# Agent attention and a max-out layer on one core: own order tables for the last two groups and the groups beside a batch border, and one more group of q turned by DMA

## The chip, the core and the metric

The kernel runs on one core of one Trainium2 chip. The metric is device time in microseconds (us) of one launch. The profile gives a span, from the first to the last instruction of the program; the measured time also holds some 2.7 us around it.

## The reference

Four batches of 12544 tokens with 128 channels go through two stages. The first is attention by way of 49 agents for each batch. The second is a feed-forward layer that takes the maximum of three products.

```python
a2k = softmax(scale * agents @ k.T)          # 49 x 12544, over the tokens
agent_v = a2k @ v                            # 49 x 128
x = softmax(scale * q @ agents.T) @ agent_v  # tokens x 128
h = max(x @ w1, x @ w2, x @ w3)              # tokens x 768
out = h @ w_out                              # tokens x 128
```

## The kernel before

**Tiles and stages.** Tokens stand in tiles of 128, 98 tiles in a batch, 392 in all. Queries go in 49 groups s of eight tiles (GT = 8). A batch ends in the middle or at the end of a group: the tiles of batch b start in group 12, 24 and 36 (`tails`). Keys and values go in groups of nine tiles (KT = 9). The keys of batch 0 are worked off first, alone. The keys of batch b are worked off beside the query groups of batch b - 1, one key group in each query group (`hosting`). The group just ahead of a border (11, 23, 35) hosts no keys. It hosts the tail of the batch instead (`k_tail`): the sum over all keys, its reciprocal, and two products that fold the agents' values into the weights (G, lines 354 to 361). Query group SB = 36 and later have no keys beside them.

**One query group** is a chain of small steps, each with a name that the tables and the prediction use:
- `load`, `cast` (POOL, line 412) and the turning of q into qT: either `qt` (eight transposes on TensorE, line 417) with `qe` (VectorE copies the result, line 422), or `turn_q_dma` (the DMA queue of SP turns it, line 428). Before the change the second way is used in groups 36 to 48 alone.
- `s` (TensorE, line 434) and `ex` (ScalarE exponentials, line 440).
- for each of six columns f of 128: `u` (TensorE, line 460), `a` (ScalarE ReLU into SBUF, line 475), `v` (TensorE, line 460) and `x` (VectorE maximum, line 485). Column 3 is different: `a3` works in place (line 472), `v3` adds to the same PSUM tile, and `x3` is a ScalarE ReLU (line 483).
- for each half o of the group: `lin` (TensorE, line 490), six `oc` (TensorE, line 499, four matmuls each, one for each column) and `sc` (VectorE scales, line 506); then `store` (SP, line 513).
- `sum` and `rec` (lines 448 and 454): the row sums of the softmax.
- of the hosted keys: `ks` (line 255), `ke` (ScalarE, line 260), `kv` (line 266), `ka` (VectorE, line 276), `kx` (POOL, line 283), and the casts of k and v on POOL (lines 223 and 230).
- of a tail: `sum_e` (VectorE, line 328), `total` (TensorE, line 333), `normalise` (VectorE, lines 339 to 342), `prod0` and `prod1` (TensorE line 354, then ScalarE line 361).

**What sets the order.** Nothing reorders at run time. Each step is put on one list by `at` with a key; group s starts at 6.0 * s, and tables of offsets give each step its key. `emit` sorts the list and issues the steps, so that each engine gets its instructions in this order. A step whose inputs are not yet issued, or for which the ring of PSUM tiles is full, is put aside and issued as soon as it can be:

```python
for op in sorted(ops, key=lambda o: o[:2]):
    if not go(op):
        late.append(op)
        continue
```

A very low offset therefore means "as soon as it can". The rings are three double-bank tiles for `u`, `v` and the products ("uv"), and two single-bank tiles for `qt`, `s`, the host tile, and both halves' outputs ("om"). A step that takes a slot waits on the engine that last read it. Table KEY is used for groups 0 to 35 and LATE for 36 to 48.

Of the kernel before, what the change touches and what calls it, by code (L numbers as in the profile page):

```python
# [16 lines left out]
def kernel(  # L17
# [19 lines left out]
    B, N, C = q.shape  # L37
# [6 lines left out]
    GT = 8  # L44
    NT = N // P
# [3 lines left out]
    NQ = B * NT // GT  # L49
    SB = (B - 1) * NT // GT  # L50
    assert NT % 2 == 0 and B * NT % GT == 0


    KEY = {
        "qt": -5.826, "qe": -4.714, "s": -3.397, "ex": -3.144, "ho": -2.653, "ks": -2.585,
        "ke": -1.395, "u0": -1.385, "u1": -0.945, "a0": -0.578, "a1": -0.505, "kv": -0.272,
        "sum": -0.189, "rec": -0.160, "ka": -0.096, "v0": -0.088, "u3": 0.041, "a3": 0.349,
        "x0": 0.448, "v1": 1.119, "v3": 1.156, "x1": 1.388, "u2": 1.556, "x3": 2.207, "u4": 2.461,
        "a2": 2.461, "v2": 2.540, "a4": 2.626, "x2": 2.904, "u5": 3.056, "v4": 3.065, "a5": 3.309,
        "x4": 3.802, "v5": 4.472, "x5": 5.223, "lin0": 6.482, "oc02": 6.840, "oc03": 7.560,  # L60
        "oc04": 8.286, "oc00": 8.460, "oc01": 8.460, "oc05": 8.461, "sc0": 8.860, "lin1": 9.007,
        "oc15": 9.269, "oc10": 9.504, "oc12": 9.761, "oc11": 11.129, "oc13": 11.301,
        "oc14": 11.651, "sc1": 11.652,
    }
    LATE = {
        "oc04": -102.316, "s": -5.143, "ex": -3.890, "ho": -3.007, "u0": -2.479, "sum": -2.401,
        "a0": -2.109, "u1": -1.115, "rec": -0.632, "u2": -0.631, "a1": -0.201, "v1": -0.150,
        "u3": 0.004, "a2": 0.202, "a3": 1.295, "x1": 1.296, "v0": 1.603, "v3": 1.692, "x0": 1.773,
        "v2": 1.787, "x3": 2.014, "x2": 2.121, "u4": 2.761, "u5": 2.826, "a4": 2.857, "v4": 3.484,
        "a5": 3.667, "v5": 3.891, "x4": 4.081, "x5": 4.963, "lin1": 6.405, "oc14": 6.642,  # L70
        "oc12": 6.780, "oc10": 8.128, "oc11": 8.220, "oc15": 8.227, "oc13": 8.498, "sc1": 8.670,
        "lin0": 9.304, "oc01": 9.553, "oc00": 9.686, "oc03": 11.369, "oc02": 11.426,
        "oc05": 11.684, "sc0": 12.804,
    }
    PRODUCT_KEYS = (-6.500, -6.260)

    const = ctx.enter_context(tc.tile_pool(name="const", bufs=1))
    loads = ctx.enter_context(tc.tile_pool(name="loads", bufs=14))
# [11 lines left out]
    def at(key, fn, name=None, needs=(), ring=None, frees=()):  # L90

        ops.append((key, len(ops), fn, name, needs, ring, frees))
# [102 lines left out]
    def keep_busy(times):  # L197
        t = small_tile("m_ps")
        for _ in range(times):
            nc.tensor.matmul(t, ident, busy, start=True, stop=True, skip_group_check=True)  # L200
# [9 lines left out]
    def k_group(b, t0, n, key, s):  # L210

        d = {}
        early = s is None

        def load():
            for name, src in (("k", k), ("v", v)):
                t = d[name] = load_tile()
                nc.sync.dma_start(t[:, :n, :], src[b, t0 * P:(t0 + n) * P, :].rearrange(
                    "(p j) c -> p j c", j=n))
# [69 lines left out]
        if early:  # L289
            g = ("early", t0)  # L290
            at(key - 30, load)
            at(key - 5, cast_k)
            at(key - 4, cast_v)
            at(key, turn_k, ("kt", g), (), "uv", [("kt_out", g)])
            at(key + 0.5, evacuate, ("kt_out", g), [("kt", g)])

            last = [("normalise", 0)] if t0 + n == NT else []
            late = max(0, (key - last_key) / 6 + 2)
            at(min(key + 6.6, last_key + 0.58 + 0.02 * late), scores, ("ks", g), [("kt_out", g)],
               "uv", [("ka", g)] + last)  # L300
            at(min(key + 7, last_key + 0.64 + 0.01 * late), exps, ("ke", g), [("ks", g)])
            done = last_key + (0.6 + 0.1 * late if late >= 1 else 0.55)
            at(min(key + 13.2, done), values, ("kv", g), [("ke", g)])
            at(min(key + 13.6, done + 0.01), add_values, ("ka", g), [("kv", g)])
        else:
            at(key + KEY["ks"] - 22, load)
            at(max(key + KEY["ks"] - 10, last_key - 3.4), cast_k)
            at(max(key + KEY["ks"] - 8, last_key - 3.3), cast_v)
            if s > 1:
                at(max(key + KEY["ks"] - 6.5, last_key - 3.2), turn_k, ("kt_out", s))  # L310
            else:

                turn = 1.2 if s else last_key + 1.05
                at(turn, turn_k, ("kt", s), (), "uv", [("kt_out", s)])
                at(turn + 0.05, evacuate, ("kt_out", s), [("kt", s)])

            at(key + KEY["ks"] if s else KEY["u0"] + 0.6, scores, ("ks", s), [("kt_out", s), ("ho", s)])
            at(key + KEY["ke"], exps, ("ke", s), [("ks", s)])
            at(key + KEY["ke"] + 1.5, add_exps, ("kx", s), [("ke", s)])
            at(key + KEY["kv"], values, ("kv", s), [("ke", s)])  # L320
            at(key + KEY["ka"], add_values, ("ka", s), [("kv", s)])

    def k_tail(b, sum_key, keys, s):
        d = {}
# [60 lines left out]
    def q_group(s):  # L385
# [3 lines left out]
        key = 6.0 * s  # L389
# [29 lines left out]
        def evacuate():  # L419
# [3 lines left out]
            else:  # L423
                nc.scalar.activation(d["qT"].rearrange("p j c -> p (j c)"), d["qT_ps"], AF.Copy)

        def turn_q_dma():
            d["qT"] = work.tile([P, GT, P], BF16, tag="qT", bufs=3, name="qT")
            nc.sync.dma_start_transpose(out=d["qT"], in_=d["qb"].rearrange("p j c -> p (j c)"))
# [83 lines left out]
            for src, r0, r1, m in rows(d["out"]):  # L512
                nc.sync.dma_start(out[r0:r1, :].rearrange("(p j) c -> p j c", j=m), src)

        K = KEY if s < SB else LATE
        new = [("product", tails[s], i) for i in range(2)] if s in tails else []

        def put(name, fn, *needs, ring=None, frees=()):
            at(key + K[name], fn, (name, s), needs, ring, frees)

        old = [(f"v{f}", s - 3) for f in range(NF)] + [("lin0", s - 3), ("lin1", s - 3),
                                                     ("sum", s - 3)] if s >= 3 else []
        if s == 0:
            at(last_key - 29.9, load)
            at(last_key - 3.5, cast)
            at(last_key + 0.82, turn_q, ("qt", 0), (), "om", [("qe", 0)])
            at(last_key + 0.825, evacuate, ("qe", 0), [("qt", 0)])
            at(last_key + 1, scores, ("s", 0), [("qe", 0)], "om", [("ex", 0)])
            at(last_key + 1.01, exps, ("ex", 0), [("s", 0)])
        elif s < SB:  # L530
            at(key + K["qt"] - 20, load)
            at(max(key + K["qt"] - 7, last_key - 3), cast)
            put("qt", turn_q, ring="om", frees=[("qe", s)])
            put("qe", evacuate, ("qt", s), *([("s", s - 3)] if s >= 3 else []))
        else:
            at(key + K["s"] - 24, load)
            at(key + K["s"] - 8, cast)
            at(key + K["s"] - 5.5, turn_q_dma, ("qe", s))
        if s:
            put("s", scores, ("qe", s), ring="om", frees=[("ex", s)])  # L540
            put("ex", exps, ("s", s), *old)
        extra = [("ka", s)] if s in hosting else [("normalise", tails[s + 1])] if s + 1 in tails else []
        if s:
            put("ho", host_tile, ring="om", frees=[("rec", s)] + extra)
        else:
            at(KEY["u0"] - 0.04, host_tile, ("ho", 0), (), "om", [("rec", 0)] + extra)
        put("sum", sums, ("ex", s), ("ho", s),
            *([("ks", s)] if s in hosting else [("total", s)] if s + 1 in tails else []))
        put("rec", recips, ("sum", s))
# [12 lines left out]
        for o in range(2):  # L562
            put(f"lin{o}", lambda o=o: out_linear(o), ("ex", s), *new, ring="om", frees=[(f"sc{o}", s)])
            for f in range(NF):
                put(f"oc{o}{f}", lambda o=o, f=f: out_hidden(o, f), (f"lin{o}", s), (f"x{f}", s))
            put(f"sc{o}", lambda o=o: out_scale(o), ("rec", s),
                *[(f"oc{o}{f}", s) for f in range(NF)], *([("store", s - 3)] if s >= 3 else []))
        at(key + max(K["sc0"], K["sc1"]) + 0.5, store, ("store", s), [("sc0", s), ("sc1", s)])

    def ramp():  # L570

# [15 lines left out]
    last_key = KEY["u0"] - 2  # L587
# [8 lines left out]
    for g, n in enumerate(first_sizes):  # L596
        k_group(0, sum(first_sizes[:g]), n, first_key + 6.0 * g, None)

        if 4 <= g < len(first_sizes) - 5:
            fillers += [(first_key + 6.0 * g + 0.55, 3), (first_key + 6.0 * g + 1.3, 3)]  # L600
    k_tail(0, last_key, (last_key + 0.95, last_key + 1.02), None)
    for key, n in fillers + [(last_key + 0.9, 2), (last_key + 1.1, 2)]:
        at(key, lambda n=n: keep_busy(n), ("busy", key), (), "om", [("busy", key)])
    tails = {b * NT // GT: b for b in range(1, B)}
    hosting = set()
    for b in range(1, B):
        for g in range(NK):
            s = (b - 1) * NT // GT + g
            hosting.add(s)
            k_group(b, g * KT, min(KT, NT - g * KT), 6.0 * s, s)  # L610
    for s, b in tails.items():
        assert s - 1 not in hosting
        k_tail(b, 6.0 * (s - 1) + KEY["ho"] + 0.001, [6.0 * s + PRODUCT_KEYS[i] for i in range(2)], s - 1)
    for s in range(NQ):
        q_group(s)
    ramp()
# [33 lines left out]
```

The softmax here doesn't subtract the row's maximum and nothing guards it: scores larger than these inputs give would overflow.

## Time and profile before

| | |
|---|---|
| time, three runs | 469.22, 469.46, 470.57 us (median 469.46) |
| the profiled execution | 470.23 us; span 467.5 us |
| TensorE busy, matmuls 5478 | 437.3 us |
| VectorE (DVE) busy | 408.3 us |
| ScalarE (ACT) busy | 396.7 us |
| POOL busy | 165.8 us |

A group of instructions on the page is written as line, engine, operation, result and inputs. The idle time behind the bar is that of the engine just before these instructions, with what ended it. TensorE's share tells little, because matmuls overlap and their ends are modelled. The chain of waits, and the timeline of a single group, tell more. From the start of one group's exponentials (line 440) to the next, the trace has these periods: 8.35 us in groups with keys, 7.83 us in groups 37 to 47, and at the three borders 10.94 (group 11), 10.94 (group 23), and 7.58 and 10.39 us (groups 35 and 36). The first group's exponentials start at 45.18 us, the last one's at 448.81 us.

### The profile page before, as it was taken

The page shows a single profiled execution, that of the slowest core. Times are in us where ns is not written, and L with a number is a line of the kernel's source. Part 1 is how long each engine was busy: PE and PEld are TensorE (multiplying, and loading weights), DVE is VectorE, ACT ScalarE, POOL GpSimd, SP SyncE. Part 2 cuts the span into 40 slices and gives each one's busy share as a digit, 9 for nine tenths or more (in the row PEclk, how much of TensorE's full clock was granted, in tenths as well). Part 3 has the DMA queues.
Part 4 walks back from the last instruction along what each step waited for, and adds up shares of the span by engine and source line. Part 5 has one row for each costly group of instructions (what it writes and reads, how often), then busy time and mean ns, then how long its engine had stood idle before and what let it go on. Part 6 is the DMA issues. An engine that isn't in the chain of part 4 may idle for free.

```text
span 467.5 us, 13338 instructions
## 1 busy us (share of the span) xinstructions
PE 437.3 (94%) x5478; PEld 273.4 (58%) x5478; DVE 408.3 (87%) x519; ACT 396.7 (85%) x461; POOL 165.8 (35%) x166
## 2 busy tenths in 40 slices
PE   2398899999999999999989999999989999999996
PEld 2376366666655666666656666666655555555554
DVE  3155699999998999999998999999988999999995
ACT  3267889989898899898989898998989999999992
POOL 3244863644460545535262446353220111010000
PEclk9999999999999999999999999999999999999999
DMA  8999999998987999987986999976365776553512
GB/s 324 397 411 405 408 289 361 315 325 215 328 277 260 285 263 328 304 266 234 314 291 225 286 335 285 275 226 192 126 114 158 215 169 183 150 145 100 105 77 105
DMA packets 79464, 117.75 MB, mean 252 GB/s; under 512 B 53223, under 2 KB 54699, under 8 KB 79403
## 3 DMA queue, kind: packets, MB, share of 16 engines
q1 hardware_dynamic: 79200, 116.80, 81.8%
q8 instruction: 42, 0.69, 0.6%
q14 instruction: 19, 0.16, 0.1%
q10 hardware_dynamic: 203, 0.10, 0.1%
HBM read 78.74 MB, written 25.69 MB: 223 GB/s over the span
## 4 chain that ended last, share of the span: by engine, by line
PE 78%; DMA 10%; DVE 6%; ACT 3%; issue 1%; POOL 0%; SPq 0%; DVEq 0%; ACTq 0%; POOLq 0%
PE uv_ps L460 33%; PE o_ps L499 28%; DMA st<-in_k_dram 7%; PE o_ps L490 6%; DVE r L485 4%; PE m_ps L417 4%; PE m_ps L434 3%; DMA wst<-in_moe_w_dram 2%; ACT a_sb L475 2%; PE m_ps L266 1%; PE m_ps L255 1%; DVE o_sb L506 1%; DMA ag_st<-in_agents_dram 1%; PE m_ps L448 1%; PE uv_ps L354 1%
## 5 line engine op out<-in xcount | busy, mean ns | idle before, releaser
L485 DVE TENSOR_TENSOR r<-uv_ps,a_sb 128x1024 bf16<-128x1024 f32 x245 | 297.3, 1220 | 13.9 <-PE uv_ps L460 4.2
L475 ACT ACTIVATE a_sb<-uv_ps 128x1024 bf16<-128x1024 f32 x245 | 241.3, 1028 | 11.5 <-PE uv_ps L460 11.1
L460 PE MATMUL uv_ps<-e_q,G 49*128 49x512 bf16 (+3 forms) x1248 | 185.5, 368 | 4.8 <-DVE r L485 2.9
L499 PE MATMUL o_ps<-wo_bf,r 128*128 128x128 bf16 x2352 | 176.4, 220 | 0.0
L499 PEld LDWEIGHTS <-r 128*128 128x128 bf16 x2352 | 137.6, 98 | 44.2 <-issue 42.7
L460 PEld LDWEIGHTS <-G 49*128 49x128 bf16 x1248 | 56.1, 93 | 66.3 <-issue 31.9
L283 POOL TENSOR_TENSOR Eacc<-Eacc,e_k 128x441 f32<-128x441 f32 (+1 forms) x30 | 30.5, 1015 | 130.5 <-ACT e_k L260 130.5
L506 DVE TENSOR_TENSOR o_sb<-o_ps,recips 128x512 f32<-128x512 f32 x98 | 67.6, 690 | 9.7 <-PE o_ps L499 6.8
L412 POOL CAST q_bf<-st 128x1024 bf16<-128x1024 f32 x49 | 51.0, 1040 | 70.6 <-DMA qT<-q_bf 68.8
L483 ACT ACTIVATE r<-uv_ps 128x1024 bf16<-128x1024 f32 x49 | 50.1, 1023 | 26.3 <-PE uv_ps L460 26.3
L223 POOL CAST k_bf<-st 128x1152 bf16<-128x1152 f32 (+2 forms) x45 | 50.4, 1119 | 28.9 <-DMA st<-in_k_dram 26.1
L472 ACT ACTIVATE uv_ps<-uv_ps 128x1024 f32<-128x1024 f32 x49 | 49.6, 1013 | 0.3 <-PE uv_ps L460 0.2
L490 PE MATMUL o_ps<-G,e_q 128*128 128x256 bf16 x196 | 38.0, 276 | 1.8 <-DVE o_sb L506 1.8
L230 POOL CAST v_bf<-st 128x1152 bf16<-128x1152 f32 (+1 forms) x33 | 37.5, 1135 | 0.5 <-DMA st<-in_v_dram 0.5
L440 ACT ACTIVATE e_q<-m_ps 128x512 bf16<-128x512 f32 x49 | 29.9, 610 | 0.5 <-PE m_ps L434 0.5
L243 DVE COPY kT<-uv_ps 128x1152 bf16<-128x1152 bf16 (+1 forms) x14 | 9.9, 709 | 17.9 <-PE uv_ps L237 17.7
L228 ACT ACTIVATE v_bf<-st 128x1152 bf16<-128x1152 f32 (+1 forms) x12 | 12.9, 1072 | 14.6 <-DMA st<-in_v_dram 14.6
L490 PEld LDWEIGHTS <-e_q 128*128 128x128 bf16 x196 | 12.8, 97 | 20.6 <-issue 20.6
L417 PEld LDWEIGHTS <-q_bf 128*128 128x128 bf16 x288 | 16.2, 98 | 14.8 <-issue 13.2
L422 DVE COPY qT<-m_ps 128x1024 bf16<-128x1024 bf16 x35 | 23.8, 681 | 0.0
L417 PE MATMUL m_ps<-ident,q_bf 128*128 128x128 bf16 x288 | 22.2, 220 | 0.8 <-POOL q_bf L412 0.8
L237 PE MATMUL uv_ps<-ident,k_bf 128*128 128x128 bf16 x116 | 11.7, 262 | 10.8 <-POOL k_bf L223 10.8
(68 smaller groups left out, 234.7 us busy)
## 6 DMA issues: line engine op xcount, KB each, us to landing
st<-in_q_dram SPq DMA_DIRECT2D x46, 512.0 KB, 4.6
out_dram<-o_sb SPq DMA_DIRECT2D x46, 512.0 KB, 3.5
st<-in_k_dram SPq DMA_DIRECT2D x40, 576.0 KB, 6.6
st<-in_v_dram SPq DMA_DIRECT2D x40, 576.0 KB, 7.4
st<-in_k_dram SPq DMA_DIRECT2D x3, 512.0 KB, 6.3
st<-in_v_dram SPq DMA_DIRECT2D x3, 512.0 KB, 7.1
wst<-in_moe_w_dram SPq DMA_DIRECT2D x3, 384.0 KB, 10.4
st<-in_q_dram SPq DMA_DIRECT2D x2, 384.0 KB, 4.2
```

The lines of the kernel that those rows point to most:

```text
L223: nc.gpsimd.tensor_copy(out=d["kb"][:, :n, :], in_=d["k"][:, :n, :])
L230: nc.gpsimd.tensor_copy(out=d["vb"][:, :n, :], in_=d["v"][:, :n, :])
L412: nc.gpsimd.tensor_copy(out=d["qb"], in_=d["q"])
L417: nc.tensor.transpose(t[:, j * P:(j + 1) * P], d["qb"][:, j, :], ident)
L460: nc.tensor.matmul(t[:, h, j0 * P:j1 * P], G[b][h * H:h * H + A, col + f * P:col + (f + 1) * P], d["e"][h * H:h * H + A, j0 * P:j1 * P], s ...
L472: nc.scalar.activation(u, u, AF.Relu)
L475: nc.scalar.activation(a_sb[f], u, AF.Relu)
L483: nc.scalar.activation(r, v_ps[f], AF.Relu)
L485: nc.vector.tensor_tensor(out=r, in0=v_ps[f], in1=a_sb[f], op=ALU.max)
L490: nc.tensor.matmul(t[:, i * 2 * C:(i + 1) * 2 * C], d["e"][:, jj * P:(jj + 1) * P], G[batch[jj]][:, C1O:C1O + 2 * C], start=(i == 0), stop ...
L499: nc.tensor.matmul(t[:, c:c + C], r_sb[f][:, h, jj * P:(jj + 1) * P], wo_bf[:, f, :], start=False, stop=True, skip_group_check=True)
L506: nc.vector.tensor_tensor(out=d["out"][:, j:j + m, :], in0=d["o", o].rearrange("p (j c) -> p j c", c=C), in1=d["r"][:, j:j + m].unsqueeze( ...
```

## The change

Three more tables are added: BORDER for the group ahead of a border (11, 23, 35), BEGIN for the group that starts a batch (12 and 24; group 36 keeps LATE), and LAST for groups 47 and 48. The numbers in KEY, LATE and PRODUCT_KEYS are replaced as well. The group ahead of a border has its q turned by the DMA queue, so three groups of `qt` and `qe` go and three DMA transposes come. Loads, casts and turns get fixed offsets instead of offsets that hang on the table, and steps after a cast name it as a need.

```diff
-    PRODUCT_KEYS = (-6.500, -6.260)
+    BORDER = {
+        "sc1": -68.143, "a4": -63.861, "oc05": -59.505, "x0": -20.368, "s": -5.286, "ex": -4.229,
...
+    }
+    BEGIN = {
+        "ex": -67.488, "oc14": -39.744, "oc10": -36.235, "sc0": -20.962, "sc1": -10.161,
...
+    }
+    LAST = {
...
+        "lin1": 6.380, "oc12": 6.800, "oc10": 7.661, "oc14": 9.630, "oc13": 13.661,
+        "oc15": 16.540, "sc1": 27.567, "lin0": 39.242, "oc00": 45.984, "oc03": 53.964,
+        "oc02": 58.314, "oc04": 63.552, "oc05": 93.035,
+    }
+    PRODUCT_KEYS = (-7.059, -3.008)
+
+    def table(s):
+        if s >= NQ - 2:
+            return LAST
+        if s + 1 in tails:
+            return BORDER
+        return BEGIN if s in tails and s < SB else KEY if s < SB else LATE
...
-            at(key + KEY["ks"] - 22, load)
-            at(max(key + KEY["ks"] - 10, last_key - 3.4), cast_k)
-            at(max(key + KEY["ks"] - 8, last_key - 3.3), cast_v)
+            at(key - 24.6, load)
+            at(max(key - 12.6, last_key - 3.4), cast_k, ("k_cast", s))
+            at(max(key - 10.6, last_key - 3.3), cast_v, ("v_cast", s))
...
+        K = table(s)
+        q_dma = s >= SB or s + 1 in tails
...
-        elif s < SB:
-            at(key + K["qt"] - 20, load)
-            at(max(key + K["qt"] - 7, last_key - 3), cast)
-            put("qt", turn_q, ring="om", frees=[("qe", s)])
+        elif not q_dma:
+            at(key - 26, load)
+            at(max(key - 12.8, last_key - 3), cast, ("q_cast", s))
+            put("qt", turn_q, ("q_cast", s), ring="om", frees=[("qe", s)])
             put("qe", evacuate, ("qt", s), *([("s", s - 3)] if s >= 3 else []))
         else:
-            at(key + K["s"] - 24, load)
-            at(key + K["s"] - 8, cast)
-            at(key + K["s"] - 5.5, turn_q_dma, ("qe", s))
+            at(key - 32, load)
+            at(key - 14.3, cast)
+            at(key - 12.3, turn_q_dma, ("qe", s))
```

## The prediction

> **What bounds the kernel now.** I read the chain of waits first, then one period in the timeline, then the places where the period is longer.
>
> ```profile
> PE 78%; DMA 10%; DVE 6%; ACT 3%; issue 1%; POOL 0%; SPq 0%; DVEq 0%; ACTq 0%; POOLq 0%
> ```
>
> TensorE carries the chain, but it is not alone. Group 18 on ScalarE:
>
> ```profile
> 203.75 1.01 ACT L472 ACTIVATE uv_ps<-uv_ps 128x1024 f32<-128x1024 f32 x1
> 205.30 1.02 ACT L483 ACTIVATE r<-uv_ps 128x1024 bf16<-128x1024 f32 x1 [0.54 <-PE uv_ps L460]
> 206.22 1.94 ACT L475 ACTIVATE a_sb<-uv_ps 128x1024 bf16<-128x1024 f32 x2
> ```
>
> Here a3 must end before v3, and v3 before x3: ScalarE idles 0.54 us in each group. The 8.35 us of a group are one loop: a4 ends and frees the slot of v4; TensorE then runs v4, 12 output matmuls, ks, v5 and u0 (1.55 us from v4 to u0); a0 follows 0.42 later; then a0, a1, a3, the wait for v3, x3, a2, a4. Spacings from the trace: 0.05 + 1.55 + 0.42 + 0.92 + 1.00 + 1.01 + 0.05 + 0.49 + 0.92 + 0.90 + 1.03 = 8.34. The border is longer (busy time by stage: TensorE, its weight loads, VectorE, ScalarE, POOL):
>
> ```profile
> 224.73:233.09 8.36, 8.36 (x110) 5.32 (x108) 8.02 (x11) 7.63 (x11) 3.09 (x3) 1.00 0.98 353
> 241.41:252.35 10.94, 9.88 (x108) 5.42 (x108) 9.29 (x14) 9.06 (x11) 1.00 (x1) 1.00 0.73 241
> ```
>
> No engine is full in the second row. ScalarE waits for first products, and these for slots that VectorE frees late, because `normalise` stands in its queue and waits for `total`:
>
> ```profile
> 242.25 1.02 ACT L475 ACTIVATE a_sb<-uv_ps 128x1024 bf16<-128x1024 f32 x1 [0.21 <-PE uv_ps L460]
> 243.99 1.02 ACT L475 ACTIVATE a_sb<-uv_ps 128x1024 bf16<-128x1024 f32 x1 [0.72 <-PE uv_ps L460]
> 245.39 1.02 ACT L475 ACTIVATE a_sb<-uv_ps 128x1024 bf16<-128x1024 f32 x1 [0.37 <-PE uv_ps L460]
> ...
> 243.00 0.48 DVE L339 RECIPROCAL m_ps<-m_ps 128x49 f32<-128x49 f32 x1 [0.41 <-PE m_ps L333]
> ```
>
> The end, VectorE and then TensorE:
>
> ```profile
> 458.38 2.36 DVE L485 TENSOR_TENSOR r<-uv_ps,a_sb 128x1024 bf16<-128x1024 f32 x2
> 460.66 0.68 DVE L506 TENSOR_TENSOR o_sb<-o_ps,recips 128x512 f32<-128x512 f32 x1
> 463.15 0.69 DVE L506 TENSOR_TENSOR o_sb<-o_ps,recips 128x512 f32<-128x512 f32 x1 [0.94 <-PE o_ps L499]
> ...
> 461.61 1.50 PE L499 MATMUL o_ps<-wo_bf,r 128*128 128x128 bf16 x24
> ```
>
> The last maximum x5(48) ends at 460.74. After that only 24 output matmuls stand before the last scaling.
>
> And the start, POOL and then TensorE:
>
> ```profile
> 45.05 1.15 POOL L230 CAST v_bf<-st 128x1152 bf16<-128x1152 f32 x1 [0.48 <-DMA st<-in_v_dram]
> 47.71 1.15 POOL L223 CAST k_bf<-st 128x1152 bf16<-128x1152 f32 x1 [1.52 <-DMA st<-in_k_dram]
> 48.80 1.04 POOL L412 CAST q_bf<-st 128x1024 bf16<-128x1024 f32 x1
> ...
> 48.07 0.39 PE L266 MATMUL m_ps<-e_k,v_bf 128*128 128x49 bf16 x9 [0.69 <-ACT e_k L260]
> ```
>
> **What the Trainium skill says.** TensorEngine Tiling (Array Packing), Key Properties: changing the tiling mode drains TensorE. The trace agrees: output matmuls start 0.056 us apart, a `u` or `v` after one starts 0.151 later, so a switch costs 0.095. TensorE: Matmul & The Clock Gate, "Wait — 56ns, not 53.3ns?", gives the same 56 ns. DMA: Bandwidth & Descriptors, "Anatomy of one DMA — SWDGE (gpsimd) path", puts most of a transfer's fixed time after the last byte; the stores here go from SP, and agree: the last one is issued at 463.86, its packets run from 464.6 to 466.15, the span ends at 467.5.
>
> **Part 1: KEY and LATE, no cost.** In the changed program's order, ScalarE and VectorE do the same steps in the same order in groups with KEY. On TensorE `s, lin1, u5, v4` becomes `s, u5, lin1, v4`: one switch more, 0.095. It is hidden, because v4 waits 0.15 for the end of a4 today. ks moves behind 12 output matmuls instead of 4, 8 x 0.056 = 0.45 later: ke can then start 1.60 us after ex, a0 0.43 later at 2.03, and a0 waits for u0 until 2.15 anyway. That cover is 0.12. LATE drops two switches (oc03 no longer splits u1 from u2), 0.19 of TensorE, but its loop of 7.83 also goes through ScalarE and VectorE (u0 waits for a4, a2 for x5), with the same steps between: nothing.
>
> **Part 2: the start, +0.8.** Because last_key rises from -3.385 to -3.067, the cast of k of group 1 now stands ahead of the cast of v of group 0 in POOL's queue. It still waits for its load until 47.71, and v(0) is cast at 47.71 + 1.09 = 48.80 to 49.95 instead of 45.05. kv(0) needs it: 50.01 instead of 48.07, and queued behind it on TensorE are sum(0), v0(0), u3(0). q of group 1 is cast 1.09 later too, so qt(1) starts at 50.99 instead of 49.90. a3(0) is 1.3 late. Group 1 has waits of its own, and one filler matmul fewer ahead of kv(1); followed step by step a3(1) comes at 59.95 instead of 59.18, and 0.77 stays.
>
> **Part 3: the borders, -4.3.** Removed in each: eight transposes (0.45 on TensorE) and a copy (0.68 on VectorE, line 422). Added: one DMA transpose, 1.6 us in SP's queue (the stores and loads behind it have over 10 us of room) and 4.4 us to landing, by the 13 that the trace has; it is cast and issued over ten key units, 14 us, ahead of `s`. Moved: sum_e ahead of x1 and normalise ahead of sc0, ex of the border group into the 0.54 gap ahead of x3, prod1 behind the next group's ex. Before, total stood behind v4 and normalise waited for it; now it is free at 6.99 us after ex(22) and VectorE reaches it at 7.10. I followed each step with the trace's spacings, in us after ex(22), before from the trace and after by the sum:
>
> - a0(23): 10.90, now 10.03. u0 waits for x2(22), which ends at 9.56, +0.05 +0.42.
> - a1(23): 12.30, now 11.12 (12 output matmuls between u0 and u1).
> - a3(23): 14.97, now 13.19. prod0 alone is ahead of it; u3 waits for x5(22), 12.63.
> - ex(24): 19.26, now 17.51. Then prod1, 0.69, ahead of a5(23).
> - a0(24): 21.42, now 20.07. This is where the normal loop goes on: -1.35.
>
> Groups 11 and 23 have the same order. At group 35, ex(37) comes 26.30 after ex(34) today and 24.7 by the same sum: -1.6. Together -4.3. Late next is u0(23), behind x2(22).
>
> **Part 4: the end, +2.9.** LAST puts lin0 and all oc0 of groups 47 and 48 behind both groups' oc1. lin0 takes a slot of the om ring that sc1 frees. oc10(47) alone now stands ahead of u4(48), which moves a4 0.2 and x5(48) 0.15 earlier, to 460.59. VectorE then does sc1(47) from 460.50 to 461.18 and sc1(48) from 461.11 to 461.80. lin0(48) starts at 461.85 and oc01(48) at 462.07; 44 matmuls x 0.056 remain, the last at 464.48; 0.26 later sc0(48) could start, but sc0(47) stands before it (464.51, spacing 0.61), so it runs from 465.12 to 465.81 instead of 463.84: +1.97. store(47) is issued 0.6 ahead of store(48), where today 2.5 us lie between them. One store's packets fill the 16 DMA engines for 1.6 us, so the second one ends about 1.0 later. No overlap of two stores is in the trace; the bounds are 0 and 1.6. I take 0.95.
>
> **The sum.** 0 + 0.8 - 4.3 + 2.9 = -0.6. Against the profiled execution's 470.23 us (span 467.5) this is 469.6; the median of the runs is 0.77 lower, so I say **468.9 us**. A difference of 0.3% (1.4 us) is about what a measurement of this kernel can tell from no change.
>
> **The rivals.**
> - The gain at the borders comes whole and the end costs less: stores overlap freely (-0.95), and the loop takes up the start's delay (-0.8): -2.35, 467.1 us. For it: the two groups after the start have idle time on both engines. Against: from group 2 on nothing is left to catch up with.
> - The loop slows with KEY (slower). ke stands just ahead of a0 and has 0.12 of cover. Thirty groups use KEY; if ks gives its result d us later than I count, each costs d - 0.12. It decides against the gain from 0.07 a group on (2.1 in all, +1.5, 471.0 us); at 0.15 it gives +3.9, 473.4 us. For it: x4, x5 and u1 hang on the same slots. Against: TensorE reaches v5 at the same time.
> - The borders give little: the tail's steps wait in another place, say u0(23) behind x2(22), and a third of 4.3 remains: +2.3, 471.8 us. Slots are short there; but ScalarE idles 1.3 us today.
> - q by DMA does nothing by itself: the turn is out of the way in both forms and the gain is all order. This changes no number; bounds -0.6 to 0 a border.
>
> **How the numbers follow.** The forecast has 0.52 and lies within 0.3%. The first rival has 0.28, faster. The two slower ones have 0.10 each, 0.20. The range takes in the first rival's end and the slow ones' beginning: 467.0 to 471.0 us.
>
> **What would show it.** In the profile after: periods of 8.35 and 7.83 as before; ex(23) between a3(22) and x3(22); ex(22) to ex(24) 17.5; cast of v(0) at 48.8 and kv(0) at 50.0; 52 matmuls of lines 490 and 499 behind the second-last pair of scalings, and the span's end 5 us or so after they end. Periods of 8.45 in the KEY groups, or borders over 18.5, would make it wrong.

## The result, and the profile after

The changed kernel takes 472.56 us (median of four runs, 472.45 to 472.86) against 469.64 us before on the same chip: a ratio of 1.006, with an interval from 1.0043 to 1.0078. It is slower, by 0.6%. The profiled execution took 472.59 us with a span of 470.8 us, 3.3 us more than the 467.5 us before. The times of these two executions differ by only 2.4 us, because 1.8 us of the time lie outside the span here and 2.7 lay outside it before. 468.9 us had been forecast.

The starts of the exponentials of each group (line 484 now, 440 before) show where the 3.3 us lie. Each row compares the two traces over one stretch.

| stretch | before | after | difference | forecast |
|---|---|---|---|---|
| start of the span to ex(2) | 63.46 | 65.88 | +2.4 | +0.8 |
| first two borders, ex(10) to ex(15) and ex(22) to ex(27) | 44.33, 44.34 | 43.90, 43.88 | -0.43, -0.46 | -1.35 each |
| third border, ex(34) to ex(38) | 34.15 | 32.78 | -1.37 | -1.6 |
| groups 38 to 47 | 78.48 | 78.60 | +0.1 | 0 |
| groups with keys away from the borders | 8.35 | 8.35 | +0.6 in all, see below | 0 |
| ex(48) to the end | 18.73 | 21.18 | +2.45 | +2.9 |

The fifth row is no slower loop. Single groups last longer once (8.66 in group 8, 8.65 in 16, 8.58 in 30; before, one of 8.63 in group 31), and all others keep 8.35. The period of the last groups is 7.86 instead of 7.83; before, a single group of 7.98 lay among them.

The line of the chain by engine, from the page:

```profile
PE 70%; DVE 11%; DMA 10%; issue 5%; ACT 3%; POOL 1%; DVEq 0%; SPq 0%; POOLq 0%; ACTq 0%
```

TensorE fell from 78 to 70%, VectorE rose from 6 to 11%, and "issue", time in which an engine waited for nothing that the profile shows, rose from 1 to 5%.

**The start.** POOL's timeline (start, duration, line, operation; the bracket is the idle time ahead of it and what ended it):

```profile
47.52 1.15 POOL L264 CAST k_bf<-st 128x1152 bf16<-128x1152 f32 x1 [3.20 <-DMA st<-in_k_dram]
48.61 1.15 POOL L271 CAST v_bf<-st 128x1152 bf16<-128x1152 f32 x1
```

As forecast, k of group 1 is cast first. POOL waits 3.2 us for its load, and v of group 0 follows at 48.6. TensorE's timeline at the same place:

```profile
46.72 0.40 PE L296 MATMUL m_ps<-agT,kT 128*128 128x49 bf16 x9
49.81 0.41 PE L307 MATMUL m_ps<-e_k,v_bf 128*128 128x49 bf16 x9 [2.70 <-POOL v_bf L271]
50.94 1.03 PE L458 MATMUL m_ps<-ident,q_bf 128*128 128x128 bf16 x8
51.77 0.63 PE L625 MATMUL o_ps<-busy,ident 128*128 128x512 bf16 x1
```

kv(0) starts at 49.81, near the forecast 50.01. What the forecast had not is in the last two lines: eight transposes take 1.03 us and a filler matmul 0.63. The same two before took 0.62 and 0.38:

```profile
49.90 0.62 PE L417 MATMUL m_ps<-ident,q_bf 128*128 128x128 bf16 x8 [0.53 <-POOL q_bf L412]
50.36 0.38 PE L582 MATMUL o_ps<-busy,ident 128*128 128x512 bf16 x1
```

The transposes start 107 ns apart instead of 56, and the next instruction comes 427 ns behind the filler, where 216 lay between two fillers before. TensorE's granted clock on record agrees (stretch, its length, TensorE's busy time and matmuls, the clock, DMA share, GB/s):

```profile
47.12:50.53 3.41, 0.72 (x17) 1.00 1.04 414
50.53:53.94 3.41, 3.41 (x26) 0.50 1.01 404
```

TensorE ran at half its clock for 3.41 us.

**The border.** Stages from ex(22) to ex(24) and from ex(24) to ex(25) (length; busy time of TensorE, its weight loads, VectorE, ScalarE and POOL with their instructions; clock, DMA share, GB/s):

```profile
235.67:253.18 17.51, 16.90 (x203) 10.79 (x202) 16.48 (x23) 16.02 (x20) 7.25 (x7) 1.00 0.93 300
253.18:262.86 9.68, 8.78 (x134) 6.33 (x131) 8.31 (x11) 8.23 (x11) 3.72 (x4) 1.00 0.96 297
```

The first stage is the forecast 17.51 to the digit. The second one is 1.3 us longer than a group with keys, and both ScalarE and TensorE are idle for a part of it. TensorE:

```profile
255.81 0.84 PE L543 MATMUL o_ps<-wo_bf,r 128*128 128x128 bf16 x12
257.55 0.39 PE L307 MATMUL m_ps<-e_k,v_bf 128*128 128x49 bf16 x9 [0.90 <-POOL v_bf L271]
257.88 0.61 PE L504 MATMUL uv_ps<-e_q,G 49*128 49x256 bf16 x8
```

VectorE, and then ScalarE:

```profile
256.70 0.69 DVE L550 TENSOR_TENSOR o_sb<-o_ps,recips 128x512 f32<-128x512 f32 x1
257.31 0.20 DVE L498 RECIPROCAL recips<-m_ps 128x8 f32<-128x8 f32 x1
```

```profile
258.59 1.01 ACT L516 ACTIVATE uv_ps<-uv_ps 128x1024 f32<-128x1024 f32 x1 [0.91 <-PE uv_ps L504]
```

kv(24) starts 0.05 us after rec(24) ends on VectorE at 257.50. v0 and u3 stand behind kv on TensorE, and a3 on ScalarE waits for u3. The bracket at kv names POOL's cast of v. That can't be the reason. The instructions of the tile v_bf, in the stretch from 255 to 259 us, have this line (its second part gives the first and the last start):

```profile
L307 PEld LDWEIGHTS <-v_bf x9: 95/96/98, 256.4 to 257.7; 128*128 128x128 bf16 x9
```

The first weights of kv(24), which are v, were loaded at 256.4, so that v was there 1.1 us before kv ran. The cast named in the bracket happens to end at the right moment and belongs to a later group.

**The end.** VectorE, and then TensorE:

```profile
458.93 2.36 DVE L529 TENSOR_TENSOR r<-uv_ps,a_sb 128x1024 bf16<-128x1024 f32 x2 [0.55 <-PE uv_ps L504]
461.20 1.28 DVE L550 TENSOR_TENSOR o_sb<-o_ps,recips 128x512 f32<-128x512 f32 x2
465.19 1.29 DVE L550 TENSOR_TENSOR o_sb<-o_ps,recips 128x512 f32<-128x512 f32 x2 [2.70 <-PE o_ps L543]
```

```profile
462.75 2.62 PE L543 MATMUL o_ps<-wo_bf,r 128*128 128x128 bf16 x44
```

The forecast picture: two scalings, 52 matmuls of lines 534 and 543 (the last 44 in one row), two more scalings, and then both stores.

### The profile page after: what moved, and what is told of

Same layout as the page of the kernel before. It is cut to its first block, busy times and chain, and to the rows that moved or that the text cites. A ratio compares the mean times of both kernels' runs of the same rounds, so it can differ in the third digit from the quotient of the medians.

```text
span 470.8 us, 13304 instructions
## 1 busy us (share of the span) xinstructions
PE 435.8 (93%) x5450; PEld 279.2 (59%) x5454; DVE 405.9 (86%) x516; ACT 397.3 (84%) x461; POOL 165.6 (35%) x166
## 4 chain that ended last, share of the span: by engine, by line
PE 70%; DVE 11%; DMA 10%; issue 5%; ACT 3%; POOL 1%; DVEq 0%; SPq 0%; POOLq 0%; ACTq 0%
PE uv_ps L504 29%; PE o_ps L543 24%; DVE r L529 9%; DMA st<-in_k_dram 7%; PE o_ps L534 5%; PE m_ps L458 4%; PE m_ps L478 3%; ACT a_sb L519 2%; DMA wst<-in_moe_w_dram 2%; PE m_ps L307 2%; PE m_ps L296 1%; DVE o_sb L550 1%; DMA ag_st<-in_agents_dram 1%; POOL v_bf L271 1%; PE o_ps L625 1%
## 5 line engine op out<-in xcount | busy, mean ns | idle before, releaser
L543 PE MATMUL o_ps<-wo_bf,r 128*128 128x128 bf16 x2352 | 169.1, 220 | 0.0
L504 PEld LDWEIGHTS <-G 49*128 49x128 bf16 x1248 | 59.3, 93 | 62.9 <-issue 35.2
L458 PEld LDWEIGHTS <-q_bf 128*128 128x128 bf16 x264 | 15.2, 99 | 13.3 <-issue 11.7
L301 ACT ACTIVATE e_k<-m_ps 128x441 bf16<-128x441 f32 (+1 forms) x33 | 17.9, 544 | 4.6 <-PE m_ps L296 1.5
L463 DVE COPY qT<-m_ps 128x1024 bf16<-128x1024 bf16 x32 | 21.8, 680 | 0.0
```

What stands on the lines that cost most here:

```text
L458: nc.tensor.transpose(t[:, j * P:(j + 1) * P], d["qb"][:, j, :], ident)
L504: nc.tensor.matmul(t[:, h, j0 * P:j1 * P], G[b][h * H:h * H + A, col + f * P:col + (f + 1) * P], d["e"][h * H:h * H + A, j0 * P:j1 * P], s ...
L543: nc.tensor.matmul(t[:, c:c + C], r_sb[f][:, h, jj * P:(jj + 1) * P], wo_bf[:, f, :], start=False, stop=True, skip_group_check=True)
```

## The experiments

Each kernel is the changed one with one edit, unless it is said otherwise. Ratios are to the kernel before, run on the same chip. Where two kernels are set against each other, the difference of their ratios is taken times 470 us.

**1. The cast of v(0) first again (e1_cast).**

```diff
-            at(max(key - 12.6, last_key - 3.4), cast_k, ("k_cast", s))
+            at(max(key - 12.6, last_key - (3.25 if s == 1 else 3.4)), cast_k, ("k_cast", s))
```

> The changed kernel, but the cast of v of group 0 stands ahead of the cast of k of group 1 in POOL's queue again. Theory A (the order of these two casts costs the start 2.4 us: kv(0) comes 1.9 us late, and TensorE, idle for 2.9 us ahead of it, then runs at half its clock): ex(1) starts 2.4 us earlier, at about 55.2, matmuls behind kv(0) stand 56 ns apart, and the time is 470.1 us. Theory B (only the lateness of kv(0) costs, as in the prediction's sum; the rest of the 2.4 comes from the other moves at the start): 0.8 us less, 471.8 us, with ex(1) at 56.8. Theory C (the start is taken up later): the time stays at 472.5 us.

Measured: 470.29 us, ratio 0.9999 (0.9984 to 1.0013). That is 0.6%, or 2.9 us, less than the changed kernel: Theory A by the time. But in the profiled execution, one of the slower ones of this kernel (471.67 us), ex(1) came at 56.80, and the transposes again stood 107 ns apart. Nine of the twelve times lay from 469.7 to 470.4 us, three from 471.4 to 472.1. So the order of the casts costs about what was thought, but the clock halves in some executions with the old order too.

**2. Fillers in the idle time (e2_fill).**

```diff
+    at(-0.3, lambda: keep_busy(12), ("busy", -0.3), (), "om", [("busy", -0.3)])
     hosting = set()
```

> The changed kernel with the late cast kept, and with twelve more filler matmuls of 512 columns (2.6 us of TensorE) put into the 2.9 us in which TensorE waits for kv(0). Nothing else moves. Theory A (half of the start's loss is the halved clock after the idle time): behind kv(0) the matmuls stand 56 ns apart instead of 107, a3(0) stays at 51.1, ex(1) comes 1.3 to 1.6 us earlier than 57.57, and the time is about 471.1 us. Theory B (lateness alone): the spacing may change, but ex(1) and the time do not (472.5 us); or kv(0) is pushed back a little and it gets 0.2 us worse.

Measured: 471.35 us, ratio 1.0022 (1.0009 to 1.0035), 1.8 us less than the changed kernel. ex(1) came at 56.32, 1.25 us earlier (1.48 if both are counted from ex(0)). TensorE's timeline:

```profile
47.18 2.75 PE L240 MATMUL m_ps<-busy,ident 128*128 128x512 bf16 x12
50.86 0.62 PE L458 MATMUL m_ps<-ident,q_bf 128*128 128x128 bf16 x8
51.32 0.38 PE L625 MATMUL o_ps<-busy,ident 128*128 128x512 bf16 x1
```

Transposes and filler have their old durations again. Work that nobody needs made the kernel faster: Theory A. kv(0) is as late as in the changed kernel (49.88), so the lateness that is left and the clock are told apart.

**3. LATE for the last two groups (e3_last).** The function `table` returns LATE instead of LAST for groups 47 and 48.

> The changed kernel, but groups 47 and 48 take their order from LATE like the groups ahead of them. Theory A (the 52 matmuls and the second pair of scalings behind the last maximum cost 2.45 us): ex(48) to the end of the span takes 18.7 us instead of 21.2, and the time is 470.1 us. Theory B (most of the loss at the end lies in the two stores that fall together): the matmuls go, but the stores still end within 1 us of before, and only 1.2 us come back, 471.3 us. Theory C (LAST gains something ahead of the end that LATE loses): under 1 us.

Measured: 470.71 us, ratio 1.0008 (0.9994 to 1.0021), 2.4 us less. From ex(48) to the end it takes 18.92 us instead of 21.18. The last two scalings of VectorE:

```profile
464.11 0.69 DVE L550 TENSOR_TENSOR o_sb<-o_ps,recips 128x512 f32<-128x512 f32 x1 [0.56 <-PE o_ps L543]
465.67 0.69 DVE L550 TENSOR_TENSOR o_sb<-o_ps,recips 128x512 f32<-128x512 f32 x1 [0.87 <-PE o_ps L543]
```

They stand apart again, and behind the last one only one store is left. Theory A.

**4. kv ahead of the row sums in groups 12 and 24 (e4_kv).**

```diff
-        "sum": -1.769, "u0": -1.331, "ke": -1.267, "a0": -1.234, "u1": -0.905, "rec": -0.514,
+        "sum": -0.341, "u0": -1.331, "ke": -1.267, "a0": -1.234, "u1": -0.905, "rec": -0.514,
```

> The changed kernel, but in groups 12 and 24 the row sums stand behind kv in TensorE's queue. Theory A (kv waits for rec, which reads the PSUM tile that kv writes, and rec waits behind x5 and sc1 on VectorE; this holds up v0, u3 and with them a3): the wait of 1.1 us ahead of kv(24) goes, a3(24) starts 0.9 us earlier, the same in group 12, and the time is 470.7 us (-1.8). Theory B (the wait moves on: x5 and sc1 are late anyway, and u3 or v0 wait for their slots instead): a3(24) gains under 0.3 us and the time stays within 0.6 us of 472.5. Theory C (rec itself comes later and holds the next group): slower than 472.5.

Measured: 471.28 us, ratio 1.0016 (1.0004 to 1.0028), 2.1 us less. The same two stages as above:

```profile
236.38:253.89 17.51, 16.89 (x203) 10.79 (x202) 16.49 (x23) 16.02 (x19) 7.26 (x7) 1.00 0.91 294
253.89:262.60 8.71, 8.71 (x134) 6.30 (x131) 8.17 (x11) 8.17 (x11) 3.72 (x4) 1.00 0.92 285
```

The second one is 0.97 us shorter, and TensorE is busy through all of it. TensorE, and then POOL:

```profile
257.20 0.39 PE L307 MATMUL m_ps<-e_k,v_bf 128*128 128x49 bf16 x9
257.44 0.24 PE L492 MATMUL m_ps<-sel,e_q 128*128 128x2 bf16 x4
```

```profile
257.12 1.15 POOL L271 CAST v_bf<-st 128x1152 bf16<-128x1152 f32 x1
```

kv no longer waits, and it runs more than 1 us before the cast ends that the bracket had named. The wait was for rec. Group 12 gives the same 0.98 us (8.71 instead of 9.69). Theory A.

**5. All three edits (e5_all).** The edits of e1_cast, e3_last and e4_kv together.

> The changed kernel with all three edits at once: cast of v(0) first again, LATE for groups 47 and 48, row sums behind kv in groups 12 and 24. Theory A (the three losses stand one behind the other on the path and add up; what is left is the gain at the borders): the ratios to the kernel before that each edit alone gave lie 0.6, 0.5 and 0.4% under that of the changed kernel, so the ratio is 0.990 to 0.992, some 466 us; borders together 4.3 us shorter than before. Theory B (the end or the start gives back what the borders gain): ratio 0.995 or more.

Measured: 465.82 us, ratio 0.9908 (0.9893 to 0.9923), span 464.0 us. Faster than both kernels, by 0.9% against the one before. ex(10) to ex(15) takes 42.91 us, ex(22) to ex(27) 42.92, ex(34) to ex(38) 32.77: 1.42, 1.42 and 1.38 under before, 4.2 together. The losses add up: Theory A.

**6. The same with six fillers (e6_fill5).**

```diff
+    for key, n in ((-0.3, 3), (0.17, 3)):
+        at(key, lambda n=n: keep_busy(n), ("busy", key), (), "om", [("busy", key)])
```

> The kernel with the three edits, and three filler matmuls of 512 columns (0.65 us) ahead of kv(0) and three ahead of qt(1), in the two idle stretches of 0.9 and 0.7 us that TensorE has there although the cast of v(0) stands first. Theory A (in some executions these stretches are enough to halve the clock, as in the profiled one with the cast alone put back, where ex(1) came 1.9 us late): ex(1) comes at about 55.0 with matmuls 56 ns apart in between, the times scatter less, and the median falls by 0.3 to 0.8 us against the three edits without fillers. Theory B (stretches under 1 us do not halve the clock; the scatter has another cause): the same time, or 0.2 us more because the fillers hold an output slot.

Measured: 466.22 us, ratio 0.9913 (0.9899 to 0.9926), no difference from 0.9908. ex(1) came at 55.58, 0.5 us later than without the fillers (55.08). The clock halved in neither profiled execution. Where there is no halving to prevent, the fillers only take time. By the granted clock on record, one of the four executions of e5_all probably had a halved start (0.995, 466.52 us) and none of e6_fill5. With so few, nothing decides between the two theories.

**7. The turn by DMA alone (e7_turn).** The kernel before, with one condition changed:

```diff
-        elif s < SB:
+        elif s < SB and s + 1 not in tails:
```

> The kernel before with one part of the change alone: q of groups 11, 23 and 35 is turned by the DMA queue instead of by TensorE and VectorE; all tables stay. Theory A (the turn is out of the way at the border in both forms, the gain there is all order): the three borders change by under 0.2 us each and the ratio to the kernel before is 0.999 to 1.000. Theory B (the eight transposes and the copy stand on the path of the border): 0.4 to 0.7 us less at each border, ratio 0.996 to 0.997.

Measured: 468.68 us, ratio 0.996 (0.9947 to 0.9973). Each border is 0.43 us shorter (10.51 instead of 10.94 twice, 7.15 instead of 7.58): Theory B. VectorE, and then TensorE; ex(22) is at 233.87 here:

```profile
240.95 0.69 DVE L506 TENSOR_TENSOR o_sb<-o_ps,recips 128x512 f32<-128x512 f32 x1
```

```profile
241.69 0.38 PE L490 MATMUL o_ps<-G,e_q 128*128 128x256 bf16 x2
```

Without the copy of line 422 (0.68) ahead of it, this scaling starts 7.08 us after ex(22) instead of 7.68. lin0 takes the slot that the scaling frees. TensorE had idled 0.60 us for it before and does not wait now.

**8. KEY at the borders (e8_key).** `table` returns KEY up to group 35 and LATE from there to 46; groups 47 and 48 keep LAST.

> The changed kernel without the tables BORDER and BEGIN: the groups on both sides of a border use KEY (LATE from 36 on); the turn of q by DMA, the new places of the two products and everything else stay. Theory A (the order of the tables makes the gain at the borders): the stretch from ex(22) to ex(27), 43.9 us in the changed kernel, 44.3 in the one before and 42.9 with the wait of kv gone, grows to 44.0 to 44.6; all three borders lose 1.5 to 2.5 us together, time 474 to 475 us. Theory B (the turn by DMA and the places of the products make it): the stretch stays at 43.9 or gets shorter, because kv does not wait for rec in KEY's order, time 471 to 472.5 us.

Measured: 478.60 us, ratio 1.0171 (1.0157 to 1.0185). ex(22) to ex(27) takes 45.39 us, ex(34) to ex(38) 35.95. Theory A has the right sign, and was too small: the borders lose 6.2 us against the changed kernel, not 1.5 to 2.5. ScalarE at the second border waits for the first product:

```profile
248.10 1.02 ACT L400 ACTIVATE G<-uv_ps 128x1024 bf16<-128x1024 f32 x1 [2.28 <-PE uv_ps L393]
```

This kernel also says something on the start. The casts stand as in the changed kernel, kv(0) waits as long, and yet TensorE's timeline has

```profile
51.24 0.62 PE L456 MATMUL m_ps<-ident,q_bf 128*128 128x128 bf16 x8
51.69 0.38 PE L623 MATMUL o_ps<-busy,ident 128*128 128x512 bf16 x1
```

with full clock. This execution was the fastest of its kernel (477.56 us, mean granted clock 1.000; the others 478.55 to 478.9, 0.993 to 0.994).

**9. The changed kernel once more (e9_again).**

> The changed kernel itself once more, with more executions. Theory A (whether the clock halves behind the late kv(0) differs from execution to execution, since with the same late cast it halved in three profiled executions and not in a fourth): the times spread over two to three levels between about 469.5 and 473 us; if the profiled one is not halved, ex(2) minus ex(0) is about 19.7 us instead of 20.96, with matmuls 56 ns apart. Theory B (the 2.9 us of idle time halve it every time): all times within 0.5 us of 472.5, and 107 ns apart in the profile again.

Measured: 472.80 us, from 471.35 to 474.24, ratio 1.0048 (1.003 to 1.0067). The profiled execution was the slowest; its clock was halved for 6.83 us, and ex(2) came 22.24 us after ex(0). The spread is as Theory A has it, but the level of 469.5 us that it names was set too low: at full clock the late kv(0), the wait of kv and the end still cost what they cost. The fastest execution, 471.35 us, is the one with a mean granted clock of 0.999; the other five have 0.990 to 0.996. With the ratio measured here in place of 1.006, the gains of experiments 1 to 4 would each be 0.6 us smaller (2.3, 1.2, 1.9 and 1.5 us). That is how far the times can be trusted; the stretches of the traces agree far better with each other (43.87 to 43.90 us at each of the first two borders in all five traces that keep the changed order there).

**10. KEY at the borders, products at their old places (e10_keyprod).** As e8_key, with PRODUCT_KEYS = (-6.500, -6.260).

> The changed kernel without BORDER and BEGIN, and with the two products of a border back at the places of the kernel before (-6.5 and -6.26). Theory A (the tables' net effect at the first two borders is nothing beyond the turn by DMA; the 1.5 us lost there with KEY and the products' new places came from those places): ex(22) to ex(27) takes 43.9 to 44.1 us, ex(34) to ex(38) about 33.7, the time is 472.5 to 474 us. Theory B (KEY's order is bad at a border in itself): ex(22) to ex(27) stays above 45 us, time over 476 us.

Measured: 486.07 us, ratio 1.0333 (1.0314 to 1.0352); ex(22) to ex(27) takes 47.23 us. The size is that of Theory B. ScalarE at the second border:

```profile
248.10 1.05 ACT L517 ACTIVATE a_sb<-uv_ps 128x1024 bf16<-128x1024 f32 x1
252.57 1.02 ACT L400 ACTIVATE G<-uv_ps 128x1024 bf16<-128x1024 f32 x1 [3.42 <-PE uv_ps L393]
```

The new KEY has a0 at 0.133 and a1 at 0.192, where the old one had -0.578 and -0.505. The products' copies into G stand at -0.5 and -0.26 on the same scale. So the new KEY puts them ahead of a0 and a1 of the border group, and ScalarE, which takes its steps in order, waits 3.42 us for the product. In e8_key the first product stands at -1.06, also ahead of a0, and the wait was 2.28. Behind the wait TensorE's clock halved as well: for 6.8 us at the first border (from 146.8), for 3.4 at each of the other two (from 256.0 and 361.8) and for 3.4 at the end (from 471.0). So 486.07 us holds both losses, and they are not told apart. KEY with both products behind a0 and a1 was not tried: shown is that the new KEY loses with the products at these two places, not that it must lose at a border.

**The start in all traces.** From ex(0) to ex(2), in us, by the order of the two casts and by the spacing of the transposes of k of group 1:

| | 56 ns apart | 107 ns apart |
|---|---|---|
| v(0) first | 18.28 (before), 18.14 (e5_all), 18.55 (e6_fill5, with fillers) | 19.65 (e1_cast), 19.49 (e7_turn) |
| k(1) first | 19.72 (e8_key), 19.48 (e2_fill, with fillers) | 20.96 (after), 20.78 (e10_keyprod), 22.07 (e3_last), 22.29 (e4_kv), 22.24 (e9_again) |

The late kv(0) by itself costs 1.2 to 1.6 us. The halved clock costs another 1.1 to 1.5 where it lasts for 3.41 us, or 2.4 to 2.8 where it lasts for 6.83 (e3_last, e4_kv, e9_again).

How often it halves can be estimated from the mean granted clock of each execution, which is on record: 3.41 us at half clock lower the mean of a span of 470 us by 0.0036. (The clock also falls behind the last matmuls, where it no longer costs anything, so each execution's span is read beside it.) The twenty executions of e3_last fall into three groups: 0.998 (four, 468.9 to 469.7 us), 0.994 to 0.996 (nine, 470.3 to 470.9) and 0.992 (seven, 471.2 to 472.0). Read in this way, the clock halved in 44 of the 51 executions with k(1) first and no fillers at the start (after, e3_last, e4_kv, e8_key, e9_again), in one of nine with fillers (e2_fill), and in 6 of 21 with v(0) first (e1_cast, e5_all, e7_turn). Of the 49 executions of the kernel before that ran beside experiments 1 to 4, 23 have 0.995 or less. Its profiled execution does not, which is a part of why the two profiles differ by more than the medians.

## Why the prediction was wrong, point by point

- **Part 1, KEY and LATE without cost: right for the loop with keys.** The period with KEY is 8.35, so the cover of 0.12 us ahead of a0 held, and the first slower rival (a loop of over 8.42) fell. What was put at nothing came to 0.7 us all the same: 0.1 in groups 38 to 47 (7.86 against 7.83) and 0.6 in single long groups, whose cause is open.
- **Part 2, the start: right path, wrong size.** v(0) was cast at 48.61 (forecast 48.8), and kv(0) came at 49.81 (50.01). a3(0), forecast 1.3 us late, came 1.4 us late (51.10 instead of 49.72). The step that failed is "0.77 stays". The sum let group 1 take up 0.5 of the 1.3. At full clock nearly nothing is taken up: counted from ex(0), a3(0) is 1.3 us late in e2_fill and 1.55 in e8_key, and a3(1) still 1.2 and 1.45. The sum also priced every later matmul with the spacings of a warm TensorE, and the halved clock added the rest. a3(1) came at 61.61, where 59.95 had been forecast, and the term of 0.8 measured 2.4. The Trainium skill (TensorE: Matmul & The Clock Gate, "What's actually happening") says that TensorE falls to half its clock after an idle window of about 3.4 us, that the window runs freely, and that the moment varies between runs. The prediction used that page for a spacing and did not ask whether the 1.9 us that it added to an idle time of 0.9 came near such a window.
- **Part 3, the borders: right to a1(24), then a wait was missed.** ex(24) came 17.51 us after ex(22) (17.51), a0(24) 20.04 (20.07). The step that failed is "this is where the normal loop goes on". BEGIN puts sum(24) ahead of kv(24); in KEY it is behind. kv writes the PSUM tile that rec reads, so now it waits for rec, and rec stands behind x5(23) and sc1(22) on VectorE. This took back 0.97 of some 1.42 us in each of groups 12 and 24 (e4_kv). Without it, e5_all has -1.42, -1.42 and -1.38, 4.2 us together, where 4.3 had been forecast. Group 36 uses LATE and hosts no keys, so the third border kept its gain in the changed kernel too.
- **Part 4, the end: right, a little large.** The second pair of scalings ends 16.86 us after ex(48) (465.19 + 1.29 - 449.62) instead of 15.03: +1.83, where 1.97 had been forecast. The stores take the other 0.62 of the 2.45, where 0.95 had been taken between bounds of 0 and 1.6. e3_last gives back 2.26 of it.
- **The rivals.** "The borders give little" (471.8 us) came nearest, in part by luck. Its mechanism was of the right kind, a step that waits in another place, but u0(23) was not the place, and half of the gain remained (2.3 of 4.3) instead of a third; the dearer start made up for it. "q by DMA does nothing by itself" was wrong: it is worth 0.43 at each border, within its bounds of 0 to 0.6. The changed kernel gains no more than this at the first two borders (43.89 in e7_turn, 43.90 and 43.88 after), because the wait of kv takes back what the tables BORDER and BEGIN add to it there. Without them the new KEY loses, at least with the products at the two places tried (e8_key, e10_keyprod).
- **The sum.** Measured 2.4 - 2.3 + 2.45 + 0.7 (single long groups and the last groups) = 3.3, as the spans have it; forecast 0.8 - 4.3 + 2.9 = -0.6. Of the difference of 3.9, some 2.0 are the wait of kv, 1.6 the start, and 0.7 the single and the last groups; the end gave 0.45 back.

## What to carry to other kernels

When a step is moved ahead of another on one engine, list who reads the tile that each of them writes. Here a matmul that writes beside a result not yet read waited for that reader (0.97 us a border), and the bracket of the profile named something else that ended at the same moment. An idle stretch that a change opens on TensorE (2.9 us here) can have a price beyond its length, and useless matmuls in it can pay. A cast whose input is still on its way should not stand in an engine's queue ahead of a cast whose input has come.

## What was not expected of the hardware

- TensorE's clock halved behind 2.9 us without a matmul (the changed kernel), and in e1_cast behind two stretches of 0.9 and 0.7 us, with 0.9 us of short matmuls between them (all from one matmul's start to the next one's). With the same 2.9 us it did not halve in e8_key, and with such short stretches not in the profiled executions of before and e5_all. A part of the reason can be read from the record. In every trace the stretch between two changes of the granted clock is a whole multiple of 3.413 us (3.41, 6.83, 20.48, 92.16 and so on), and these marks fall at other places of the program in each execution. In the changed kernel nearly all of the idle time lay between two marks (47.12 and 50.53, busy for 0.72 us). In e8_key, counted on from its last change of clock, a mark at 48.70 divides it:

```profile
45.29:48.70 3.41, 2.19 (x28) 1.00 1.02 410
48.70:52.12 3.42, 1.87 (x30) 1.00 1.03 408
```

How idle such a window has to be stays open: behind one with 2.26 us of busy time (e1_cast, 46.65 to 50.06) the clock fell, and behind 1.87 us here it did not. The page named above speaks of an idle window of about 3.4 us that runs freely. The multiples of 3.413 us and the variation between runs agree with it, but windows that were idle only in part were enough here. For a cold TensorE the same page ("Wait — 56ns, not 53.3ns?") gives spacings of 106.7 and 426.7 ns, and 107 and 427 were measured.

- Single groups are longer by 0.2 to 0.3 us, at the same place in different kernels: 8.65 to 8.67 in group 8, 8.62 to 8.65 in group 16 and 8.57 to 8.58 in group 30 of the changed kernel and of all its variants that keep its tables at the borders. In group 8 of the changed kernel, x5 starts 0.36 us later after ex than in group 9 (2.37 instead of 2.01). The bracket names the matmul v5, but the matmuls of line 504 around it start 1.51 us after ex in both groups. The cause is open.
